# Attention and soft mixture of experts in one kernel: the loads of the values split by head instead of by batch

## The chip, the core and the metric

The kernel runs on one core of one Trainium2 chip. The metric is the device time of one execution, in microseconds (us). A core has five engines that run side by side: PE (TensorE, matrix multiplies), DVE (VectorE), ACT (ScalarE), POOL (GpSimd) and SP (SyncE), which here does nothing but issue transfers. Sixteen DMA engines move the data of all transfers. In this kernel transfers are issued by POOL and by SP, and each of the two has a queue of its own: in the profile q0 ("software_dynamic") is POOL's queue and q1 ("hardware_dynamic") is SP's.

## The reference, cut to what matters

```python
batch, n_heads, seq, head_dim = (8, 12, 448, 64)          # q, k, v, float32

scores = scale * np.matmul(q, k.transpose(0, 1, 3, 2))
m = np.max(scores, axis=-1, keepdims=True)
e = np.exp(scores - m)
attn = e / (np.sum(e, axis=-1, keepdims=True) + np.exp(-m) + 1e-09)
out = np.matmul(attn, v)
...
x = out.transpose(0, 2, 1, 3).reshape(B * S, H * D)        # 3584 x 768
logits = x @ phi                                          # 768 x 32
d = softmax(logits over the rows);  c = softmax(logits over the slots)
slot_input = d.T @ x                                      # 8 experts x 4 slots
slot_out[e] = np.maximum(slot_input[e] @ w1[e], 0.0) @ w2[e]
return c @ slot_out
```

The second half is written here in short: the two softmaxes are those of the reference, with the maximum taken off first and 1e-9 added to the sum.

## The kernel before, in words

**Units.** The attention is done in 24 units. Unit `u` is a pair of batches (`bp`, four of them) and a pair of heads (`hp`, six of them). The 448 rows of a sequence are cut into 64 groups of 7 consecutive rows (`P = 64`, `TB = 7`). Batch 0 of the pair stands on partitions 0 to 63 and batch 1 on partitions 64 to 127. A partition holds, for each of the two heads, its group of 7 rows, which are 7 x 64 = 448 consecutive float32 numbers (1792 bytes) in memory.

**Loads.** `load` (L95) fills such a tile with two transfers, one per batch: 64 partitions, two heads each, 448 numbers a head. Queries and keys are loaded so by POOL's queue (`load_qk`, L102), which turns them into bf16 on the way. They have one raw buffer each, and unit 0 has a place of its own. The values are loaded so as float32 (`load_v`, L108): unit 0 by POOL's queue, all others by SP's. There is one raw buffer for the values (`vr`). The weights of the experts come by POOL's queue, 768 KB in each of 32 transfers (`load_w`, L129).

**What the values go through.** `stage_V` (L248) has POOL cast the raw values to bf16 (L250) and set a column of ones beside them (L252). The result, of which there are two buffers, is what the AV matmuls (`stage_AV`, L271) multiply with. As there is one raw buffer, the load for unit u + 1 can start when L250 of unit u has read it.

**The rest of a unit.** `stage_T` (L188) transposes queries and keys, `stage_S` (L200, L204) makes the scores a first time and L208 (DVE) takes their maxima. `stage_MT` turns the maxima round, and POOL writes them out by L220 and L226. `stage_ST` (L236, L241) makes the scores again, transposed and with the maximum taken off, and ACT takes the exponential (L245). `stage_AVout` copies the product away (L281, L284), `stage_den` (L290, L291) and `stage_N` (L297, L299) divide by the sum, and `stage_X` (L345, L347) transposes the result for the mixture. At the end of each pair of batches come the logits and the slot sums, and at the end of all the two matmuls of the experts and 28 output tiles of 384 KB, which SP's queue stores (L670).

**What sets the order.** The order is written out by hand. A counter `n` runs over the steps, 7 to a unit. At each step the program issues one pair of score matmuls of `stage_S`, one step of `stage_ST` for the step 10 before (`LAG`), and what a table (`plan`, filled by `at(n, where, ...)`) holds for that step. For unit u, whose first step is n = 7u, the table holds among others: at n + 3 the transposes of unit u + 1 and the loads of queries and keys of unit u + 2; at n + 5 the load of a weight (units 2 to 22, two of them in units 9 and 16); at n + 7 `stage_MT`; at n + 9 the cast of the values (`stage_V(u)`) and right behind it the load of the values of unit u + 1; from n + 13 to n + 18 the AV matmuls; at n + 19, n + 20 and n + 22 `stage_AVout`, `stage_den` and `stage_N`. Each engine does its instructions in the order in which the program issues them. So on POOL, what stands behind a cast waits for it, the issues of the transfers too.

Before the first step the program issues, in this order, the queries and keys of unit 0, an identity matrix, the queries and keys of unit 1, some constants, and `load_v(0)`.

Of the kernel before, what the change touches and what calls it, by code (L numbers as in the profile page):

```python
# [16 lines left out]
P = 64  # L17
# [6 lines left out]
def kernel(  # L24
# [10 lines left out]
    nc = tc.nc  # L35
# [7 lines left out]
    TB = S // P  # L43
    KC = DD // 128
    FK = F // 128
    HP = H // 2
# [8 lines left out]
    gdma = nc.gpsimd.dma_start  # L55
# [25 lines left out]
    def buf(name, i):  # L81
        o, n, bufs = parts[name]
        return block[:, ds(o + (i % bufs) * n, n)]
# [8 lines left out]

    RAW, V65 = {}, {}

    def load(u, t_, src, eng):  # L95
        bp, hp = divmod(u, HP)
        for b in range(2):
            eng.dma_start(out=t_[ds(b * P, P), :, :],  # L98
                          in_=src[bp * 2 + b, ds(hp * 2, 2)].rearrange("h (p t) d -> p h (t d)", t=TB))
        return t_  # L100

    def load_qk(u):  # L102

        for i, (src, name) in enumerate(((q, "qr"), (k, "kr"))):
            t_ = buf(name, 0) if u else wres[:, WRES - 1, ts(i, N2)]
            RAW[u, name] = load(u, t_.rearrange("p (h n) -> p h n", h=2), src, nc.gpsimd)

    def load_v(u):  # L108
        t_ = buf("vr", 0).bitcast(F32).rearrange("p (h n) -> p h n", h=2)
        RAW[u, "vr"] = load(u, t_, v, nc.sync if u else nc.gpsimd)  # L110

    W = {}

# [4 lines left out]
    def load_w(i):  # L118
# [11 lines left out]
        for j in range(J):  # L130
            W[kind, e, half * J + j] = t_[:, j, :]

    load_qk(0)


    ident32 = const.tile([128, 128], F32, name="ident32")
    make_identity(nc, ident32)
    ident = const.tile([128, 128], BF16, name="ident")
    nc.vector.tensor_copy(ident, ident32)
    load_qk(1)  # L140
    ones = const.tile([128, P], BF16, name="ones")
    nc.vector.memset(ones, 1.0)
# [3 lines left out]
    for base in (0, -P):  # L146
        nc.gpsimd.affine_select(
            out=nmask, in_=nmask, compare_op=ALU.not_equal, fill=-1.0,
            base=base, pattern=[[-1, TB]], channel_multiplier=1)
    load_v(0)  # L150
    M = [const.tile([128, 128], BF16, name=f"m{i}") for i in range(2)]
    for i in range(2):
# [411 lines left out]
    for u in range(U):  # L564
        n = u * TB
        if u + 1 < U:
            at(n + 3, "value", lambda u=u: [stage_T(u + 1, name) for name in ("qr", "kr")])
        if u + 2 < U:
            at(n + 3, "load", lambda u=u: load_qk(u + 2))
        at(n + 7, "value", lambda u=u: stage_MT(u))  # L570
        at(n + 9, "load", lambda u=u: stage_V(u))
        if u + 1 < U:
            at(n + 9, "load", lambda u=u: load_v(u + 1))
        for m in sorted(set(AV0)):
            at(n + m, "value", lambda u=u, m=m: [
                stage_AV(u, [t for t in range(TB) if AV0[t] == m], part) for part in range(2)])
        if u < U - 1:
            at(n + 19, "small", lambda u=u: stage_AVout(u))
            at(n + 20, "value", lambda u=u: stage_den(u))
            at(n + 22, "small", lambda u=u: stage_N(u))  # L580
        else:
            at(n + 11, "load", lambda u=u: last_sinks(u))
            at(n + 19, "small", lambda u=u: stage_last(u))
        if u < U - 2:
            at(n + 26, "value", lambda u=u: stage_X(u))
        else:
            at(n + (24 if u == U - 2 else 26), "end", lambda u=u: stage_X(u))
# [113 lines left out]
```

## Time and profile before

| what | value |
| --- | --- |
| time, median of 3 runs | 343.98 us (342.94 to 346.65) |
| time of the profiled execution | 345.78 us |
| its span in the profile | 344.0 us |
| mean TensorE clock granted | 0.928 of full |
| busy: PE / DVE / ACT / POOL | 289.1 / 255.8 / 207.5 / 202.8 us |
| casts of the values (L250) | 24, of 927 ns; the first at 20.2 us, the last at 270.3 us |
| transfers of the values | 2 by POOL's queue, 46 by SP's, 224 KB each |
| moved by all transfers | 59.09 MB, mean 172 GB/s |

The span runs from the first to the last instruction of the profiled execution; its own time is 1.8 us longer. "Busy" is the time in which an engine did work. In a row such as "L250 POOL CAST ... x24 | 22.3, 927 | 1.0 <-DMA" the parts are: the line of the kernel, the engine, the operation, its operands, the number of instructions, their time together in us, the mean of one in ns, and the idle time of the engine just before them with what ended most of it. A row of the timeline begins with its start in us and its length in us. A row of a queue gives packets, MB, and the time that its packets took as a share of sixteen DMA engines' time.

The timeline gives POOL's casts some 10 to 12.6 us apart, which is the time of one unit. Between two of them POOL issues two transfers of queries, two of keys and, in most units, one of weights.

### The profile page before, as it was taken

The page shows a single profiled execution, that of the slowest core. Times are in us where ns is not written, and L with a number is a line of the kernel's source. Part 1 is how long each engine was busy: PE and PEld are TensorE (multiplying, and loading weights), DVE is VectorE, ACT ScalarE, POOL GpSimd, SP SyncE. Part 2 cuts the span into 40 slices and gives each one's busy share as a digit, 9 for nine tenths or more (in the row PEclk, how much of TensorE's full clock was granted, in tenths as well). Part 3 has the DMA queues.
Part 4 walks back from the last instruction along what each step waited for, and adds up shares of the span by engine and source line. Part 5 has one row for each costly group of instructions (what it writes and reads, how often), then busy time and mean ns, then how long its engine had stood idle before and what let it go on. Part 6 is the DMA issues. An engine that isn't in the chain of part 4 may idle for free.

```text
span 344.0 us, 13196 instructions
## 1 busy us (share of the span) xinstructions
PE 289.1 (84%) x5864; PEld 161.7 (47%) x5864; DVE 255.8 (74%) x352; ACT 207.5 (60%) x327; POOL 202.8 (59%) x317
## 2 busy tenths in 40 slices
PE   2689999999999999987989979899989856858770
PEld 1335555555555565554655545465555433422110
DVE  2999898999889899988789979789877156016440
ACT  3037787777686677866677758676778840104340
POOL 8356676788767877767767866577636842200000
PEclk9999999999999999999999999999999985895555
DMA  6664799878898979988596999887864599945997
GB/s 87 115 99 93 138 195 168 166 160 156 169 196 143 210 147 197 194 155 160 106 193 129 215 200 150 149 155 147 163 147 84 108 182 216 214 84 207 396 399 281
DMA packets 30056, 59.09 MB, mean 172 GB/s; under 512 B 4048, under 2 KB 22224, under 8 KB 30000
## 3 DMA queue, kind: packets, MB, share of 16 engines
q0 software_dynamic: 19344, 36.69, 61.6%
q1 hardware_dynamic: 10656, 21.57, 19.0%
q8 instruction: 46, 0.75, 0.9%
q14 instruction: 10, 0.08, 0.1%
HBM read 83.46 MB, written 11.01 MB: 275 GB/s over the span
## 4 chain that ended last, share of the span: by engine, by line
PE 58%; ACT 14%; DMA 11%; DVE 8%; issue 5%; POOL 1%; SPq 0%; ACTq 0%; DVEq 0%; POOLq 0%
PE av L271 16%; PE ps L200 11%; PE ps L236 11%; PE ps L241 8%; ACT block L245 7%; PE ps L188 7%; DMA block<-in_moe_w_dram 6%; DVE m L208 5%; DMA out_dram<-wres 4%; ACT block L281 4%; ACT block L284 2%; PE ps L665 1%; DMA wres<-in_k_dram 1%; PE ps L429 1%; PE ps L212 1%
## 5 line engine op out<-in xcount | busy, mean ns | idle before, releaser
L208 DVE TENSOR_REDUCE m<-ps 128x2 bf16<-128x896 f32 x168 | 181.7, 1095 | 25.0 <-PE ps L200 21.9
L245 ACT ACTIVATE block<-ps 128x896 bf16<-128x896 f32 x168 | 154.0, 918 | 64.5 <-PE ps L241 58.5
L271 PE MATMUL av<-block 64*128 64x65 bf16 (+1 forms) x2688 | 82.8, 193 | 6.3 <-ACT block L284 2.3
L271 PEld LDWEIGHTS <-block 64*128 64x128 bf16 (+1 forms) x2688 | 70.0, 97 | 33.4 <-ACT block L284 9.5
L236 PE MATMUL ps<-block,ones 64*64 64x448 bf16 x672 | 69.1, 368 | 2.3 <-ACT block L245 0.9
L241 PE MATMUL ps<-block 64*64 64x448 bf16 x672 | 66.2, 352 | 1.9 <-issue 1.9
L220 POOL TENSOR_TENSOR block<-mt,nmask 128x768 bf16<-128x768 bf16 x24 | 35.2, 1466 | 45.9 <-ACT mt L214 43.6
L200 PE MATMUL ps<-block 64*128 64x448 bf16 x288 | 54.0, 372 | 3.3 <-DVE m L208 0.9
L200 PEld LDWEIGHTS <-block 64*128 64x128 bf16 x288 | 18.2, 94 | 55.2 <-issue 54.6
L299 POOL TENSOR_TENSOR block<-block,rec 128x896 bf16<-128x896 f32 x23 | 38.7, 1681 | 1.5 <-DVE rec L297 1.5
L98 POOL DMA_DIRECT2D block<-in_q_dram x46 | 29.4, 643 | 7.1 <-PE ps L188 6.8
L191 DVE COPY block<-ps 128x896 bf16<-128x896 bf16 x48 | 27.8, 616 | 4.4 <-PE ps L188 4.4
L236 PEld LDWEIGHTS <-ones 64*64 64x64 bf16 x672 | 25.6, 105 | 10.0 <-issue 2.9
L98 POOL DMA_DIRECT2D block<-in_k_dram x46 | 27.9, 626 | 2.3 <-issue 2.3
L188 PE MATMUL ps<-ident,block 128*64 128x128 bf16 x644 | 26.3, 229 | 3.2 <-issue 2.3
L188 PEld LDWEIGHTS <-block 128*64 128x64 bf16 x644 | 21.8, 114 | 5.7 <-issue 4.7
L241 PEld LDWEIGHTS <-block 64*64 64x64 bf16 x672 | 23.6, 107 | 0.4 <-issue 0.3
L665 PE MATMUL ps<-wres,cT 32*128 32x384 bf16 x56 | 19.1, 500 | 4.9 <-DVE wres L668 3.5
L250 POOL CAST block<-block 128x896 bf16<-128x896 f32 x24 | 22.3, 927 | 1.0 <-DMA block<-in_v_dram 1.0
L668 DVE COPY wres<-ps 128x768 f32<-128x768 f32 x14 | 13.4, 958 | 11.7 <-PE ps L665 8.4
L347 DVE COPY block<-ps 128x896 bf16<-128x896 bf16 x24 | 14.8, 616 | 9.6 <-PE ps L345 9.6
L668 ACT COPY wres<-ps 128x768 f32<-128x768 f32 x14 | 11.1, 799 | 14.7 <-DMA out_dram<-wres 9.8
(112 smaller groups left out, 241.3 us busy)
## 6 DMA issues: line engine op xcount, KB each, us to landing
wres<-in_moe_w_dram POOLq DMA_DIRECT2D x23, 768.0 KB, 9.0
out_dram<-wres SPq DMA_DIRECT2D x28, 384.0 KB, 4.7
block<-in_v_dram SPq DMA_DIRECT2D x46, 224.0 KB, 5.1
block<-in_moe_w_dram POOLq DMA_DIRECT2D x9, 768.0 KB, 13.6
block<-in_q_dram POOLq DMA_DIRECT2D x46, 112.0 KB, 4.4
block<-in_k_dram POOLq DMA_DIRECT2D x46, 112.0 KB, 5.4
block<-in_v_dram POOLq DMA_DIRECT2D x2, 224.0 KB, 4.4
wres<-in_q_dram POOLq DMA_DIRECT2D x2, 112.0 KB, 3.3
```

Source lines behind the costliest of these rows:

```text
L98: eng.dma_start(out=t_[ds(b * P, P), :, :], in_=src[bp * 2 + b, ds(hp * 2, 2)].rearrange("h (p t) d -> p h (t d)", t=TB))
L188: nc.tensor.transpose(ps[ds(h * D, D), :, ds(t * P, P)], r[:, h, ds(t * D, D)], ident)
L191: nc.vector.tensor_copy(t_, ps)
L200: nc.tensor.matmul(ps[:, h, ds(0, S)], QT[u][hs, b, ds(c * 128, 128)], KT[u][hs, b, :], start=True, stop=True)
L208: nc.vector.tensor_reduce(m[:, :, s], ps[:, :, ds(0, S)], axis=AX.X, op=ALU.max)
L220: nc.gpsimd.tensor_tensor(md[:, :, ds(0, C3 * 128)].rearrange("p b (c n) -> p b c n", c=C3), mt.unsqueeze(1).unsqueeze(1).broadcast_to([12 ...
L236: nc.tensor.matmul(ps[ds(b * P, P), h, ds(0, S)], ones[hs, :], MD[u][hs, b, :], start=True, stop=False)
L241: nc.tensor.matmul(ps[ds(b * P, P), h, ds(0, S)], KT[u][hs, b, ds(t * P, P)], QT[u][hs, b, :], start=False, stop=True)
L245: nc.scalar.activation(et, ps[:, :, ds(0, S)], AF.Exp, scale=scale)
L271: nc.tensor.matmul(o, et[bs, h, ds(c * 128, w)], V65[u][bs, h, t, ds(0, 65)], start=(t == 0 and h == 0 and c == 0), stop=(t == TB - 1), sk ...
L299: nc.gpsimd.tensor_tensor(x.rearrange("p s (h d) -> p h s d", h=2), xv[:, :, :, ds(0, D)], rec.unsqueeze(3).broadcast_to([128, 2, TB, D]), ...
L668: (nc.vector.tensor_copy if i % 2 else nc.scalar.copy)(o.rearrange("p (g n) -> p g n", g=2), ps[:, :, ds(0, 384)])
```

## The change

The values are no longer loaded by `load`. `load_v` issues two transfers of its own, one per head: each takes the rows of both batches and goes to one half of the free dimension of all 128 partitions. All of them, unit 0's too, go by SP's queue. The bytes, the layout in the buffer and everything behind it stay as they are. Queries and keys are loaded as before, and `load` loses its parameter for the engine.

```diff
-    def load(u, t_, src, eng):
+    def load(u, t_, src):
         bp, hp = divmod(u, HP)
         for b in range(2):
-            eng.dma_start(out=t_[ds(b * P, P), :, :],
-                          in_=src[bp * 2 + b, ds(hp * 2, 2)].rearrange("h (p t) d -> p h (t d)", t=TB))
+            gdma(out=t_[ds(b * P, P), :, :],
+                 in_=src[bp * 2 + b, ds(hp * 2, 2)].rearrange("h (p t) d -> p h (t d)", t=TB))
         return t_
...
-            RAW[u, name] = load(u, t_.rearrange("p (h n) -> p h n", h=2), src, nc.gpsimd)
+            RAW[u, name] = load(u, t_.rearrange("p (h n) -> p h n", h=2), src)

     def load_v(u):
         t_ = buf("vr", 0).bitcast(F32).rearrange("p (h n) -> p h n", h=2)
-        RAW[u, "vr"] = load(u, t_, v, nc.sync if u else nc.gpsimd)
+        bp, hp = divmod(u, HP)
+        for h in range(2):
+            nc.sync.dma_start(
+                out=t_[:, h, :],
+                in_=v[ds(bp * 2, 2), hp * 2 + h].rearrange("b (p t) d -> b p (t d)", t=TB))
+        RAW[u, "vr"] = t_
```

In the built program the two sides of a transfer of the values are, from the outermost step to the innermost: before, 64 x 2 x 448 in memory and 64 partitions x 2 x 448 in the buffer; after, 2 x 64 x 448 in memory and 128 partitions x 448 in the buffer.

## The prediction

> **What bounds the kernel now.** I read the page's slices and chain first. For three quarters of the span TensorE, VectorE and ScalarE take turns (the chain: PE 58%, ACT 14%, DVE 8%) at a clock of 0.9 or more; no transfer of the values is among the larger links of that chain. Then I read the transfers: the page's queues and issues, and what the values' tile view says of issue to landing.
>
> ```profile
> span 344.0 us, 13196 instructions
> ...
> q0 software_dynamic: 19344, 36.69, 61.6%
> q1 hardware_dynamic: 10656, 21.57, 19.0%
> ...
> PE 58%; ACT 14%; DMA 11%; DVE 8%; issue 5%; POOL 1%; SPq 0%; ACTq 0%; DVEq 0%; POOLq 0%
> ...
> L250 POOL CAST block<-block 128x896 bf16<-128x896 f32 x24 | 22.3, 927 | 1.0 <-DMA block<-in_v_dram 1.0
> ...
> block<-in_v_dram SPq DMA_DIRECT2D x46, 224.0 KB, 5.1
> ```
>
> ```profile
> DMA to landing us min/median/max: 3.3/5.0/8.2
> ```
>
> L250 is the only reader of the values' one raw buffer, and in the whole run it waited 1.0 us for them, once: today the values are free. Section 3 is the warning beside it: the queues' packets take 61.6% + 19.0% of sixteen engines' time, so the engines have little room, and what matters is how a transfer is shared among them.
>
> How much slack the values have is seen in the timeline of POOL and of SP's queue over one unit, from one cast to the next:
>
> ```profile
> 126.29 0.92 POOL L250 CAST block<-block 128x896 bf16<-128x896 f32 x1
> 127.16 0.15 POOL L252 MEMSET block<- 128x14 bf16 x1
> 127.21 1.29 POOL L98 DMA_DIRECT2D block<-in_q_dram  x2
> 128.48 1.22 POOL L98 DMA_DIRECT2D block<-in_k_dram  x2
> 129.64 0.62 POOL L129 DMA_DIRECT2D wres<-in_moe_w_dram  x1
> ...
> 134.57 1.68 POOL L299 TENSOR_TENSOR block<-block,rec 128x896 bf16<-128x896 f32 x1
> 136.20 0.93 POOL L250 CAST block<-block 128x896 bf16<-128x896 f32 x1
> ```
>
> ```profile
> 127.24 11.36 SPq L98 DMA_DIRECT2D block<-in_v_dram  x4
> ```
>
> The loop of the values is: cast (126.29), issue by SP (127.24, which is 0.95 later, after the memset), landing, next cast (136.20). From issue to next cast there are 9.0 us, and a load takes about 5 to 8. A load of more than 9 us makes this loop the bound of the unit: everything behind the cast on POOL (the next query and key issues, a weight issue, L220, L299) waits with it, and so do the AV matmuls of L271 that read the cast's output. Note also that POOL issues queries, keys and weights in the 3 us after the cast, that is, beside the values' transfer and nowhere else.
>
> **The change, part by part.** Bytes, packets and issue count of the values stay: two transfers of 128 packets of 1792 bytes a unit. SP's waits stay the same in kind: the first transfer waits for the memset L252 and the landing before, the second for the second landing before; neither is a new stall, because the cast has already waited for both. What moves:
>
> 1. Unit 0's values go from POOL to SP's queue. POOL loses two issues (1.23 us at 7.32), ahead of 4.35 us in which it waits for L188: worth nothing. SP has nothing to wait for, so these packets now run beside the first queries and keys, which the first transposes wait for.
>
> 2. All 48 transfers change shape. Before, both sides begin with the same step: 64 rows by 64 partitions. After, the built program has a source of 2 batches x 64 rows x 448 elements and a destination of 128 partitions x 448. This is the step on which all depends: among how many engines are the 128 packets divided? The trace cannot say, for all its transfers begin with 64 or 128 on both sides. What it shows is that each transfer ends in 16 small packets (10656 packets on q1 are 74 transfers x (128 + 16)), so today all have 16 shares. Bounds: 16 shares of 8 packets as now, or 2 shares of 64. I take 2. An engine's share has to be a start and a few steps on each side; the shares are most simply cut from the outermost step, and 2 and 128 can be cut alike into 2 pieces only. This is a choice from the form of the two patterns. The other end stays as a rival.
>
> The Trainium skill, "DMA: Bandwidth & Descriptors", section "Why a DMA increments its semaphore by 16 and not by 1", says that a copy runs on the largest number of engines up to 16 that divides the slowest step longer than one on both sides, and on SP's path takes the lowest-numbered engines. By that rule both transfers get the same two engines, and the sum is the one below; no run here shows it yet.
>
> **The sum for two engines.** Both transfers of a unit on the same two engines: 128 packets for each of the two, instead of 16. Durations from the trace's packet records: a values packet takes 74 ns with nothing beside it and 87 ns when it alternates with a packet of POOL's queue; a query or key packet 88 ns, a weight packet 474 ns. The end of the run agrees with the first: there the stores run alone,
>
> ```profile
> DMA packets 2847, 7.76 MB, mean 388 GB/s; under 512 B 322, under 2 KB 322, under 8 KB 2847
> ...
> q1 hardware_dynamic: 2847, 7.76, 98.5%
> ```
>
> 388 / 16 = 24.3 GB/s per engine, and 1792 bytes at that rate are 74 ns. In those records the two queues' packets take turns end to end on an engine, so their times add.
>
> From the cast of unit 0 (20.2 us) to that of unit 23 (270.3 us) there are 23 rounds of the loop, now 250.1 us. On a busy engine these rounds then hold:
> - values: 128 packets, about 40 of them alternating: 88 x 74 + 40 x 87 = 10.0 us; x 23 = 230 us
> - queries and keys, 21 loads of 4 transfers of 8 packets per engine: 21 x 32 x 88 ns = 59 us
> - weights, 23 loads of 8 packets per engine: 23 x 8 x 474 ns = 87 us
> - the fixed part: 0.95 from cast to issue, and the least landing of 3.3 less its own 8 packets (0.6), 2.7: 3.65 x 23 = 84 us
>
> Sum 460 us, 20.0 a round, against 250.1: **+210 us**. Nothing hides it, since the loop is closed by a single raw buffer; TensorE's some 10 us of work per unit now lies inside the wait. Part 1 adds to the start: keys of unit 0 have 32 packets an engine queued up to the last of theirs, each now with a values packet between: 32 x 87 ns = 2.8 us. The tail behind the last cast (270.3 to 344) I leave as it is; its clock of 0.5 to 0.8 could rise after the longer waits or fall further, and I put 10 us either way.
>
> The profiled execution took 345.78 us (span 344.0), 0.5% above the median of 343.98, so I add the 213 us to the median: **557 us**.
>
> Bounds. By the window from 20 to 270 us, packets cost more than the bare ones:
>
> ```profile
> q0 software_dynamic: 15552, 28.52, 66.6%
> q1 hardware_dynamic: 6624, 10.55, 14.9%
> ```
>
> q0 took 66.6% of 250 = 166 us per engine there (bare: 59 + 87 = 146), and q1 0.149 x 250 x 16 / 5888 = 101 ns a values packet. With these: 297 + 166 + 84 = 547, or +297 and 644 us; but the stretch comes from sixteen engines running at once, and here fourteen would idle, so I stand near the bare end. At the low end all at 74 ns, 10 us off the tail: 343.98 + 198 + 3 - 10 = 535 us.
>
> **The rivals.**
> - *Sixteen shares, not slower.* If the division goes by rows, each engine gets its 8 packets per transfer as now, the load stays at 5 to 8 us, under the 9.0 from which it decides, and the cast goes on waiting for nothing. What is left is the start: 16 packets an engine x 74 ns = 1.2 us at most ahead of the first queries. 344 to 346 us, no change. For it: every transfer of the trace has 16 shares. Against: none of them has unequal outer steps. The skill's same page, "Rules for kernel authors", advises one 128-partition transfer in place of two to partition halves, which speaks for the change; by it the time would be this rival's at the worst.
> - *Two shares, but the two transfers on different pairs of engines.* 64 packets an engine: 40 x 87 + 24 x 74 = 5.3 us, x 23 = 121; with 146 and 84 that makes 351, or +101, and 448 us with the start. For it: nothing in the trace fixes which engine gets a share. Against: successive transfers on one queue look alike in it.
> - *Packets of the two queues overlap on an engine.* Then only the values count: 23 x (9.5 + 3.65) = 302, or +52, 399 us. Against: the alternating packets end to end.
>
> That the transfers do not go "to all 128 partitions" at full width is the forecast itself.
>
> **How the numbers follow.** Two shares on the same engines 0.77, most of it between 510 and 620; sixteen shares 0.15; different pairs 0.06; overlap 0.02. The range must reach past the forecast's own case to the pairs: 440 to 620, leaving out the sixteen shares and the overlap. A difference of 1% is about what a measurement of this kernel tells from none. The slower cases are 0.85 and a sixth of the sixteen-share one (start not hidden): 0.87; within 1% 0.10; faster by over 1% 0.03, should the cast or the start come earlier than I see.
>
> **What would show it.** Right: L250 waiting some 9 us a unit for the values, most of the chain in DMA block<-in_v_dram, about 20 us between casts, the values' landing at 17 to 19 us, the mean DMA share falling although q1's bytes stay, long gaps of TensorE at L271. If L250 waits for nothing and landing stays near 5 us, the division was into sixteen. A landing near 10 to 12 us means four engines or overlap.

## The result

The changed kernel takes **553.95 us** (median of 6 runs, 551.54 to 555.79) against 344.1 us (6 runs) of the kernel before: a ratio of 1.607, 95% interval 1.601 to 1.613. The prediction was 557 us, slower. The profiled execution took 551.54 us, with a span of 549.7. Every ratio compares only executions in the chip's faster state, and each experiment with its own new runs of the kernel before, so a ratio can differ a little from the quotient of the medians given.

The page of the changed kernel, the lines that answer to those shown of before (queues, chain, the cast, the issues; L250 of before is L255 now, L98 of the values is L112):

```profile
span 549.7 us, 13197 instructions
...
q0 software_dynamic: 19216, 36.23, 40.2%
q1 hardware_dynamic: 10272, 22.02, 10.9%
...
DMA 83%; issue 5%; DVE 3%; PE 2%; POOL 2%; SPq 2%; ACT 1%; POOLq 0%; DVEq 0%; ACTq 0%
DMA block<-in_v_dram 75%; DMA block<-in_moe_w_dram 4%; DMA out_dram<-wres 3%; SPq L112 2%; DMA wres<-in_k_dram 2%; DVE m L213 1%; DVE wres L673 1%; POOL block L257 1%; PE ps L670 1%; POOL block L255 1%; PE av L276 1%; POOL wres L98 0%; ACT block L250 0%; PE ps L647 0%; DVE block L196 0%
...
L255 POOL CAST block<-block 128x896 bf16<-128x896 f32 x24 | 22.3, 930 | 248.0 <-DMA block<-in_v_dram 248.0
...
block<-in_v_dram SPq DMA_DIRECT2D x48, 224.0 KB
```

Three readings. The chain, which was PE 58%, is now DMA 83%, three quarters of the span in the values' transfers alone. The cast, which waited 1.0 us for the values in the whole run, waits 248.0. And the number of packets on q1 settles how the transfers are divided. 10272 packets are 48 x 128 of the values, 28 x 128 of the stores, and 544 small ones that end the transfers. Were there sixteen to each transfer, as before, they would be 76 x 16 = 1216. 544 is 28 x 16 + 48 x 2: sixteen for a store, **two for a transfer of the values**. (The last line of the view gives no time to landing.)

The loop of the values, in the timelines of POOL and of SP's queue:

```profile
281.83 0.93 POOL L255 CAST block<-block 128x896 bf16<-128x896 f32 x1 [11.64 <-DMA block<-in_v_dram]
282.71 0.15 POOL L257 MEMSET block<- 128x14 bf16 x1
282.76 1.28 POOL L98 DMA_DIRECT2D block<-in_q_dram  x2
284.01 1.22 POOL L98 DMA_DIRECT2D block<-in_k_dram  x2
285.18 0.62 POOL L134 DMA_DIRECT2D wres<-in_moe_w_dram  x1
...
289.72 1.68 POOL L304 TENSOR_TENSOR block<-block,rec 128x896 bf16<-128x896 f32 x1
301.50 0.93 POOL L255 CAST block<-block 128x896 bf16<-128x896 f32 x1 [10.10 <-DMA block<-in_v_dram]
```

```profile
282.79 20.74 SPq L112 DMA_DIRECT2D block<-in_v_dram  x4
```

It is the same loop as before, with 0.96 us from cast to issue (0.95 before), but now 18.7 us from issue to the next cast (9.0 before), of which POOL stands 10 idle. From the first cast (24.72 us) to the last (474.9) it is 450.2 us, 200.1 more than before. The start gives 4.5 us more (first cast at 24.72 against 20.2), the tail 1.1 (74.8 against 73.7). Together they are the 205.7 us between the spans.

### The profile page after: what moved, and what is told of

Its sections match the earlier page's. It is cut to its first block, busy times and chain, and to the rows that moved or that the text cites. A ratio compares the mean times of both kernels' runs of the same rounds, so it can differ in the third digit from the quotient of the medians.

```text
span 549.7 us, 13197 instructions
## 1 busy us (share of the span) xinstructions
PE 350.1 (64%) x5864; PEld 184.4 (34%) x5864; DVE 260.9 (47%) x352; ACT 208.6 (38%) x327; POOL 203.1 (37%) x315
## 3 DMA queue, kind: packets, MB, share of 16 engines
q1 hardware_dynamic: 10272, 22.02, 10.9%
## 4 chain that ended last, share of the span: by engine, by line
DMA 83%; issue 5%; DVE 3%; PE 2%; POOL 2%; SPq 2%; ACT 1%; POOLq 0%; DVEq 0%; ACTq 0%
DMA block<-in_v_dram 75%; DMA block<-in_moe_w_dram 4%; DMA out_dram<-wres 3%; SPq L112 2%; DMA wres<-in_k_dram 2%; DVE m L213 1%; DVE wres L673 1%; POOL block L257 1%; PE ps L670 1%; POOL block L255 1%; PE av L276 1%; POOL wres L98 0%; ACT block L250 0%; PE ps L647 0%; DVE block L196 0%
## 5 line engine op out<-in xcount | busy, mean ns | idle before, releaser
L250 ACT ACTIVATE block<-ps 128x896 bf16<-128x896 f32 x168 | 154.0, 918 | 234.4 <-PE ps L246 228.1
L276 PE MATMUL av<-block 64*128 64x65 bf16 (+1 forms) x2688 | 102.6, 219 | 111.7 <-POOL block L257 111.1
L276 PEld LDWEIGHTS <-block 64*128 64x128 bf16 (+1 forms) x2688 | 88.2, 114 | 149.2 <-issue 119.7
L255 POOL CAST block<-block 128x896 bf16<-128x896 f32 x24 | 22.3, 930 | 248.0 <-DMA block<-in_v_dram 248.0
L241 PE MATMUL ps<-block,ones 64*64 64x448 bf16 x672 | 85.6, 459 | 1.4 <-ACT block L250 0.5
L246 PE MATMUL ps<-block 64*64 64x448 bf16 x672 | 82.3, 444 | 0.0
L205 PE MATMUL ps<-block 64*128 64x448 bf16 x288 | 63.9, 443 | 2.5 <-DVE m L213 0.9
L193 PE MATMUL ps<-ident,block 128*64 128x128 bf16 x644 | 29.1, 234 | 38.1 <-DMA block<-in_k_dram 34.1
L196 DVE COPY block<-ps 128x896 bf16<-128x896 bf16 x48 | 29.3, 620 | 42.0 <-PE ps L193 41.9
L98 POOL DMA_DIRECT2D block<-in_q_dram x46 | 29.4, 643 | 12.1 <-PE ps L193 10.1
L241 PEld LDWEIGHTS <-ones 64*64 64x64 bf16 x672 | 27.6, 117 | 10.0 <-issue 3.7
L246 PEld LDWEIGHTS <-block 64*64 64x64 bf16 x672 | 28.7, 127 | 0.0
L98 POOL DMA_DIRECT2D block<-in_k_dram x46 | 28.0, 628 | 0.0
L352 DVE COPY block<-ps 128x896 bf16<-128x896 bf16 x24 | 14.8, 616 | 12.4 <-PE ps L350 12.4
L219 ACT COPY mt<-ps 128x128 bf16<-128x128 bf16 x24 | 6.3, 264 | 32.3 <-PE ps L217 31.5
```

What stands on the lines that cost most here:

```text
L98: gdma(out=t_[ds(b * P, P), :, :], in_=src[bp * 2 + b, ds(hp * 2, 2)].rearrange("h (p t) d -> p h (t d)", t=TB))
L193: nc.tensor.transpose(ps[ds(h * D, D), :, ds(t * P, P)], r[:, h, ds(t * D, D)], ident)
L196: nc.vector.tensor_copy(t_, ps)
L205: nc.tensor.matmul(ps[:, h, ds(0, S)], QT[u][hs, b, ds(c * 128, 128)], KT[u][hs, b, :], start=True, stop=True)
L241: nc.tensor.matmul(ps[ds(b * P, P), h, ds(0, S)], ones[hs, :], MD[u][hs, b, :], start=True, stop=False)
L246: nc.tensor.matmul(ps[ds(b * P, P), h, ds(0, S)], KT[u][hs, b, ds(t * P, P)], QT[u][hs, b, :], start=False, stop=True)
```

## The experiments

Each is a change to the changed kernel unless it says otherwise. "Loop" is the time from the first cast to the last in the profiled execution: 250.1 us before, 450.2 changed.

**Four transfers, by head and by batch.**

```diff
         for h in range(2):
-            nc.sync.dma_start(
-                out=t_[:, h, :],
-                in_=v[ds(bp * 2, 2), hp * 2 + h].rearrange("b (p t) d -> b p (t d)", t=TB))
+            for b in range(2):
+                nc.sync.dma_start(
+                    out=t_[ds(b * P, P), h, :],
+                    in_=v[bp * 2 + b, hp * 2 + h].rearrange("(p t) d -> p (t d)", t=TB))
```

> The values still go by SP's queue and still by head, unit 0 included, but each head's load is cut again by batch: four transfers a unit of 64 partitions, 64 rows on both sides. Theory (the outermost step of 2 leaves two shares, on the same two engines): 64 rows give sixteen shares again, 4 packets an engine and transfer, so the loss of 210 us is gone: 344 to 347 us, L250's successor waits for nothing, and q1 holds 96 x 16 + 28 x 16 small packets. Rival (the cut by head, or SP carrying unit 0, costs by itself): the time stays well over 400 us.

Measured: 348.28 us, a ratio to before of 1.007 (1.003 to 1.011). The queue, from the page of this kernel:

```profile
q1 hardware_dynamic: 11712, 22.03, 20.2%
```

11712 packets are 48 x 128 + 28 x 128 + 124 x 16: sixteen shares again. The loss is gone, although the values are still cut by head and unit 0 still goes by SP's queue. Each transfer fills 64 partitions here, so this run alone does not say whether the partitions or the outermost step decide; the next two do. Two things were not quite as expected: the median lies 1 us above the range, and the cast waited 6.5 us for values, in three rounds, where none was expected. How two more transfers a unit cost this was not looked into.

**Equal sides, but 62 rows.** This separates two readings of "the outermost step": that the sides of the transfer begin with unequal numbers, or that the numbers have no large common divisor.

```diff
-        for h in range(2):
-            nc.sync.dma_start(
-                out=t_[:, h, :],
-                in_=v[ds(bp * 2, 2), hp * 2 + h].rearrange("b (p t) d -> b p (t d)", t=TB))
+        for b in range(2):
+            for lo, n in ((0, 62), (62, P - 62)):
+                nc.sync.dma_start(
+                    out=t_[ds(b * P + lo, n), :, :],
+                    in_=v[bp * 2 + b, ds(hp * 2, 2)].rearrange("h (p t) d -> p h (t d)", t=TB)[ds(lo, n)])
```

> The values are cut by batch as in the kernel before, with both heads in a transfer, but the 64 rows are cut into 62 and 2: four transfers a unit, and both sides of each begin with the same step, 62 or 2. Theory (the number of shares is the largest number up to 16 that divides the outermost steps): 62 has 2 as its largest such divisor, so both kinds have two shares, 128 packets a unit fall on two engines as in the changed kernel, and the time is the changed kernel's, 545 to 565 us; q1 holds 96 x 2 + 28 x 16 = 640 small packets. Rival (shares are lost only because the two sides begin with unequal steps): sixteen shares or nearly so, 344 to 350 us.

Measured: 559.19 us, a ratio of 1.622 (1.612 to 1.632). Queue and cast, from the page of this kernel:

```profile
q1 hardware_dynamic: 10368, 22.02, 11.2%
...
L256 POOL CAST block<-block 128x896 bf16<-128x896 f32 x24 | 22.3, 930 | 258.0 <-DMA block<-in_v_dram 258.0
```

10368 - 9728 packets of data = 640 = 96 x 2 + 28 x 16. Cut by batch, as before the change, with equal sides, the values are as slow as in the changed kernel. So the loss needs neither the cut by head, nor unequal sides, nor 128 partitions in a transfer; what the two kernels have in common is the divisor.

**57 and 7 rows.** The same edit with 57 in place of 62.

> As the kernel with rows cut into 62 and 2, but into 57 and 7. Theory: 57 gives three shares and 7 gives seven, so the busiest engines get 2 x (38 + 2) = 80 packets a unit instead of 128: 40 x 87 + 40 x 74 ns = 6.4 us instead of 10.0, 23 x 3.6 = 83 us less than the changed kernel, about 471 us. Rival of unequal sides: 344 to 350 us. If any odd number of rows merely falls to two shares: about 554 us.

Measured: 458.2 us, a ratio of 1.327 (1.320 to 1.335).

```profile
q1 hardware_dynamic: 10656, 22.02, 14.0%
```

10656 - 9728 = 928 = 48 x 3 + 48 x 7 + 28 x 16, as expected for three shares of 57 rows and seven of 7. The loop is 355.8 us, 94.4 less than the changed kernel's. If the shares of both kinds begin at the same engine, the busiest engine has 48 packets a unit less, so one of these packets is worth 94.4 / (23 x 48) = 86 ns. The expectation had counted 75, and the time is 13 us under the 471 us that it gave.

**A second queue.** The first head by SP's queue, the second by ACT's.

```diff
-            nc.sync.dma_start(
+            (nc.scalar if h else nc.sync).dma_start(
```

> The changed kernel, but the second head's transfer goes by ACT's queue, the first by SP's. Theory (each queue gives a transfer's two shares to the same two engines): still 128 packets a unit on those two, 545 to 570 us. Rival (each queue or transfer has its own pair): 64 packets an engine, 5.3 us instead of 10.0, about 448 us.

Measured: 556.17 us, a loop of 452.5 us. The two queues, from the page of this kernel:

```profile
q1 hardware_dynamic: 7152, 16.52, 8.2%
q10 hardware_dynamic: 3120, 5.51, 2.6%
```

q10 is ACT's: 24 x 128 packets of data and 48 = 24 x 2 small ones. There are two queues, and not a microsecond is won; a pair of engines for each would have come out near 448 us. The time alone does not settle it, for ACT, which has to wait for the cast before it can issue, now stands 203.7 us at that place. The packet records of the trace do. The two transfers are issued together, as in this round (one row from SP's timeline, one from ACT's):

```profile
206.16 0.50 SPq L112 DMA_DIRECT2D block<-in_v_dram  x1
206.17 0.51 ACTq L112 DMA_DIRECT2D block<-in_v_dram  x1
```

Yet in the whole loop never more than two packets of the values run at a time, those of both queues taken together, but for overlaps of under 20 ns at their ends. The same holds for the two transfers of a unit in the changed kernel. So both transfers have the same two engines.

**One weight load.** Of the 23 weight loads of the attention, 22 are left out; the experts are computed with one load's data for all of them.

```diff
-        t_ = room(i).rearrange("p (j n) -> p j n", n=n)
-        gdma(out=t_, in_=src)
+        t_ = room(0 if i < WRES else i).rearrange("p (j n) -> p j n", n=n)
+        if i == 0 or i >= WRES:
+            gdma(out=t_, in_=src)
```

> The changed kernel with 22 of the 23 weight loads of the attention left out (one load's data stands for all 23, so the experts are computed with wrong weights; the number of instructions of the other engines is the same). Theory (packets of both queues take turns on the two engines, and their times add): 22 x 8 packets x 474 ns = 83 us less, about 471 us, rounds of about 16.4 us. Rival (they overlap, and the values alone set the round): 550 to 554 us.

Measured: 465.14 us (471 expected); loop 367.4, which is 82.8 us less (83 expected). The packets of POOL's queue add to those of the values on the two engines, as the alternating records of before had suggested.

**Two raw buffers.** The values of odd units get a place of their own, and the load runs two units ahead. One weight load lands where another did, so one slice of the experts' weights is wrong.

```diff
-        t_ = buf("vr", 0).bitcast(F32).rearrange("p (h n) -> p h n", h=2)
+        raw = wres[:, 21, ds(0, 2 * N2)] if u % 2 else buf("vr", 0)
+        t_ = raw.bitcast(F32).rearrange("p (h n) -> p h n", h=2)
...
+        i = 20 if i == 21 else i
...
-        if u + 1 < U:
-            at(n + 9, "load", lambda u=u: load_v(u + 1))
+        if u + 2 < U:
+            at(n + 9, "load", lambda u=u: load_v(u + 2))
...
     load_v(0)
+    load_v(1)
```

> The changed kernel with a second raw buffer for the values, and each load issued one unit earlier; one weight load lands in the place of another, so one slice of the experts' weights is wrong, with the same traffic. Theory (a round is the packets of two engines, 16.4 us, and a fixed 3.65 us that the single buffer leaves open): the fixed part is hidden, 84 us less, about 470 us. Rival (the two engines are the only bound, and the fixed part is already filled by POOL's packets): 545 to 554 us.

Measured: 456.46 us (470 expected); loop 355.9, which is 94.3 less (84 expected). The wait that the single buffer leaves open is real. But 94.3 us are 4.1 us a round, more than that wait: in the packet records of the changed kernel a round has 2.7 us from the cast to the first packet of the values and 0.5 from the last one to the next cast, 3.2 together or 73 us in the loop. Some 6 us of the rest are packets that fell out of the loop: with unit 1 loaded ahead of it there are 5729 of the values, not 5888. The other 15 us were not looked into. With all of it hidden the kernel is still a third slower than before.

**By POOL's queue.** The same two transfers, issued by POOL right behind the cast.

```diff
-            nc.sync.dma_start(
+            gdma(
```

> The changed kernel's transfers of the values, issued by POOL instead of SP, in the same place of the order, right behind the cast. Now all loads are in one queue, values ahead of queries, keys and weights of the same round. If two shares go to the same two engines: 128 packets and the others' 6.35 us fill the two engines for 15.8 us a round, about 459 us. If two shares go to changing engines: 64 packets x 74 ns + 3.65 = 8.4 us, under the 9.0 of slack, 344 to 365 us. If sixteen shares: 344 to 350 us. The theory of the pattern's divisor names no engine for POOL's queue, so it allows the first two.

Measured: 377.57 us, a ratio of 1.103 (1.091 to 1.114); loop 282.2 us. From the page of this kernel, transfers, POOL's queue and the issues:

```profile
DMA packets 40968, 59.27 MB, mean 157 GB/s; under 512 B 18832, under 2 KB 31216, under 8 KB 40912
...
q0 software_dynamic: 36880, 47.42, 69.0%
...
L112 POOL DMA_DIRECT2D block<-in_v_dram x48 | 41.1, 857 | 6.9 <-POOL block L257 4.1
```

The packet records show why there are so many. The values are now 2016 packets of 5376 bytes and 96 of 1792, which is 48 transfers x 2 shares x (21 packets of three rows and one of one row). Beside them stand 14112 packets of 12 bytes. That is 48 x 14 x 21, which would fit a tiny packet for each large one on each of the fourteen engines without a share; the records do not name the engine. So POOL's queue, too, cuts into two. The time was not foreseen: it lies between the two cases (459 for a fixed pair, 344 to 365 for changing ones), nearer to the second. The packet records show that the pairs differ: for 79 us of the loop, overlaps of under 20 ns left out, four of the large packets run side by side, where the changed kernel never has more than two. Part of what is still lost can be seen: these issues take POOL 857 ns each, ahead of those of queries and keys, and TensorE waits 18.3 us for queries. The 32 us by which the loop is longer than before were not divided further.

**Unit 0 on SP's queue, alone.** The kernel before with one word changed.

```diff
-        RAW[u, "vr"] = load(u, t_, v, nc.sync if u else nc.gpsimd)
+        RAW[u, "vr"] = load(u, t_, v, nc.sync)
```

> The kernel before with one part of the change alone: the values of unit 0 go by SP's queue, split by batch as all the others. Theory: the packets run beside the first queries and keys, at most 16 packets x 74 ns = 1.2 us later start, POOL's two issues of 1.23 us gone from a stretch in which it waits anyway: 343.5 to 345.5 us, no change. Rival (the start is a good part of the loss): over 348 us.

Measured: 342.53 us, a ratio of 0.998 (0.994 to 1.003): no difference. That part of the change is worth nothing by itself.

## Why the prediction was right

**The division (part 2).** This was a choice between two ends, argued from the form of the two patterns, and it decided everything. It is now shown: two ends per transfer in the changed kernel, and two, three or seven where 62 and 2, 57 or 7 rows lead on both sides. The argument was a little too narrow, though. It spoke of what 2 and 128 can be cut into alike; 62 and 62 could be cut alike into 62, and yet there are two shares. The rows of the runs fit a rule by divisors up to sixteen: 64 gives 16, 62 gives 2, 57 gives 3, 7 gives 7, 2 beside 128 gives 2. The Trainium skill, "DMA: Bandwidth & Descriptors", section "Why a DMA increments its semaphore by 16 and not by 1", states this rule, with the lowest-numbered engines on the SP and ACT queues. The counts 544, 640 and 928 agree with the number, and the second queue's run, with its 556 us and its two packets at a time, agrees with the same engines for both; their numbers no trace here shows.

**The same two engines.** The rival of different pairs (448 us) fell with the time and with the packet records, in which never more than two packets of the values run side by side.

**Sixteen shares, not slower.** It fell with the 544 small packets.

**Overlap.** The rival of 399 us fell: taking 22 weight loads away took 82.8 us.

**The terms of the sum**, against the 213 us that were added to the median:
- *The loop*, foreseen at 460 us, took 450.2, or 19.6 a round against 20.0. Rounds that lack a term give its size. In the run with one weight, one round has neither queries and keys nor a weight:

```profile
362.75 0.93 POOL L256 CAST block<-block 128x896 bf16<-128x896 f32 x1 [5.52 <-DMA block<-in_v_dram]
375.48 0.93 POOL L256 CAST block<-block 128x896 bf16<-128x896 f32 x1 [5.81 <-DMA block<-in_v_dram]
```

It takes 12.7 us. By the packet records 10.0 of them lie between the start of the first packet of the values and the end of the last, as foreseen, and the other 2.7 are the fixed part (3.65 foreseen). Queries and keys add 3.1 a round (2.8 foreseen), for in the changed kernel the last two rounds, which have none, take 16.5 us against 19.6. A weight adds 3.8 (82.8 / 22), as foreseen, but the loop holds 24 of them, not 23: 23 go to `wres` and one to `block`. The sum is then 23 x 10.0 + 21 x 3.1 + 24 x 3.8 + 23 x 2.7 = 230 + 65 + 91 + 62 = 448 us. So the fixed part was too large by 22 us: the least landing of the trace, less its packets, is longer than what the loop has to wait for. Queries and keys were too small by 6 us and weights by 4. The 10.0 of the values agrees in part by chance: the forecast had 40 slower packets in it that stand beside others, and this round has none.

The queue's row does not give the price of a packet. In the window of the loop it is

```profile
q1 hardware_dynamic: 5980, 10.55, 6.7%
```

and 0.067 x 450.2 x 16 / 5888 is 82 ns, which would make 241 us. But the records of an engine overlap a little: where the values run alone, packets of 74 ns begin 70 to 71 ns after one another on each of the two engines.
- *The start*, 2.8 us foreseen, took 4.5. In the values by batch (unit 0 on SP's queue alone) the first cast is at 20.7 us, 0.5 later than before, so nearly all of it is the division, not the queue. The term was taken on the two engines' packets alone and was too small by 1.7 us.
- *The tail*, put at 10 us either way, moved by 1.1.

The errors of the loop's terms have both signs, so it came out only 10 us too long; start and tail, too small by 1.7 and 1.1, take back 3 of these, and the profiled execution of the changed kernel happened to be the fastest of six. That the forecast came within 3 us of the median is thus in part luck. The mechanism is not: the two shares, the two engines and the addition of the queues' packets are each shown.

**What would show it**: the wait of L255 was foreseen at some 9 us a unit (10.8 measured), the time between casts at about 20 (19.6), the landing at 17 to 19 us after the issue (18.7 to the cast). Long gaps of TensorE at the AV matmuls came too: they wait 111.1 us for the column of ones behind the cast (L257).

## What to carry to other kernels

Before a transfer is reshaped, look at the outermost step of both its sides in the built program, not at the partitions it fills: the number of DMA engines that move it here was the largest number up to sixteen that divides both, so 2 x 64 rows to 128 partitions got two engines where 64 rows got sixteen. On SP's and ACT's queues the small packets that end a transfer told the number of its shares; on POOL's they did not. And where a buffer is alone in its loop, look how long a load may take before its reader waits, here some 9 us from issue to cast: loads of 5 to 8 us left the cast almost without a wait, and a load of 18.7 us was paid for in each round.

## What the runs showed of the hardware that I had not expected

The clock granted to TensorE was lower in the kernel in which it had to wait. The windows of the two loops (length, busy time and number of instructions of each engine, granted clock, share of the DMA engines, GB/s), first before, then changed:

```profile
20.20:270.30 250.10, 233.01 (x5244) 137.45 (x5239) 216.27 (x274) 182.97 (x282) 178.10 (x273) 1.00 0.83 159
```

```profile
24.70:475.00 450.30, 292.75 (x5252) 159.60 (x5248) 221.93 (x275) 186.45 (x285) 179.71 (x274) 0.77 0.47 88
```

It is 1.00 before and 0.77 after, and the same matmuls are busy for 293 us instead of 233. Here it can have cost little, since TensorE has only 2% of the chain that ended last; what it would cost where TensorE is near the bound was not tried. Of the prediction's pieces this concerns only the tail, whose clock lay between 0.50 and 0.86 in both kernels.

The second is POOL's queue. With two shares in a transfer it moved 14112 packets of 12 bytes beside the data, gave the two transfers of a unit different pairs of engines where SP's and ACT's queues gave the same pair, and took 857 ns to issue a transfer where one of queries takes 643 in the kernel before.
